# An attention and FFN kernel: the intermediate gh moved by 64 bytes, and a hand-written order for VectorE and ScalarE in the A stages

## The chip, the cores and the metric

One core of one Trainium2 chip. The metric is the device time of one execution in microseconds (us), the median of several runs. Five engines are named: TensorE (PE, with PEld for its weight loads), VectorE (DVE), ScalarE (ACT), GpSimd (POOL) and SyncE (SP), whose queue issues the DMAs.

## The reference

An attention over a small memory, and then a bilinear feed-forward:

```python
# q, k, v: (8 batches, 8 heads, 576, 64); phi: (8, 8, 576, 32)
a = softmax(phi, axis=2)                      # over the 576 positions
k_m = einsum('bhsm,bhsd->bhmd', a, k)         # 32 memory slots a head
v_m = einsum('bhsm,bhsd->bhmd', a, v)
attn = softmax(q @ k_m.T / sqrt(64)) @ v_m
x = attn.transpose(0, 2, 1, 3).reshape(4608, 512)
h = (x @ w1) * (x @ w2)                       # 1024 wide
out = (h @ w3) @ w_out                        # (4608, 512)
```

## The kernel before

All matmuls of the FFN work on numbers split in two fp32r halves, hi and lo, and use three products (hi·hi, lo·hi, hi·lo). `split` makes the halves: ScalarE casts the hi one, VectorE subtracts to get the lo one.

*Start.* w3 and w_out are multiplied once into W (1024x512; L493), kept as `Wh`, `Wl`.

*Attention of a batch* is cut into steps, each a generator in `attention(b)`. Heads are taken in pairs. `top` (L193) reduces `ph`, the transposed phi (two column groups t of 576), to the negated maxima `mx`. `exp` (L200) exponentiates `ph` and sums it. `norm` takes the reciprocals. `row` turns the maxima (L207), sends them to DRAM in four small DMAs (L210) and reads them back into all partitions as `all` (L212). `less` adds `all` to the rows of phi (L220, 128x1024, and L223) and exponentiates them (L226). Either these rows or, in early batches (b under `BY_ROWS` = 3), `ph` transposed on TensorE (`turn0` with eight transposes, L240, copied by ScalarE at L244; `turn4` with a ninth, L247, copied at L249) give the phi for `mem`, which multiplies it with k and v (L259, L268). Both parts of `turn` use the one PSUM tile `x`. `blocks` lays k_m and v_m out (L285 to L290). The scores, their softmax (`sc`, `se`, `sn`, `pr`) give the attention weights `ah`, `al`. `memory_weights` folds v_m into w1 and w2 and gives `mh`, `ml`, so that x is never formed.

*The A stage* of a batch: 16 units, one for each of 8 blocks f of 128 hidden features and 2 halves n of the 576 tokens. A unit is six matmuls of 288 columns into PSUM bank a (x @ w1) and six into bank b (x @ w2) (L583); a copy of a into `a_sb` on ScalarE (L597); the product `gr` = b · a_sb on VectorE (L600); and the split of `gr` into `gh[f]` (L131, ScalarE) and `gl[f]` (L133, VectorE). Banks a and b are two deep, as are `a_sb` and `gr`.

*The O stage*: for each 128 tokens 24 matmuls of 512 columns, `gh`, `gl` as weights and `Wh`, `Wl` moving (L612), a copy to `osb` (L624) and a DMA out. In all 36 blocks, so 864 matmuls. Odd batches use columns 0 to 575 of `gh` and `gl`, even batches those from 64 on.

*The order.* `START` orders the start and batch 0 step by step; then `SECOND` orders batch 1 and `STEADY` batches 2 to 7. A word is one step: `A` a unit, `O` a quarter of an output block, `top`, `less` and so on those steps for the next batch, with `+` for the one after that; `phi2`, `rows2`, `kv2` in batch 1 are loads for batch 3, and so on. TensorE and SP run always in the order of these tables. VectorE and ScalarE do so in `START` only; in `SECOND` and `STEADY` a scheduler that estimates times places their instructions. The tiles of the O and A stages (`gh`, `gl`, `a_sb`, `gr`, `turned`, `osb`) lie in pool `big`, one behind the other, `mx32` first.

Of the kernel before, what the change touches and what calls it, by code (L numbers as in the profile page):

```python
# [8 lines left out]
F32 = mybir.dt.float32  # L9
F32R = mybir.dt.float32r  # L10
# [3 lines left out]
AF = mybir.ActivationFunctionType  # L14
ALU = mybir.AluOpType
AX = mybir.AxisListType
# [27 lines left out]
pr0.1 O2 M3 M3 pr1.1 pr0.1 pr1.1 O3 O2 M3 O2 O3 O3 O3 O3 O3  # L44
""".split()
SECOND = """
phi2 A top exp A norm A turn0 A turn4 A mem rows2 A kv2 blocks A top+ row+ A exp+ A norm+ A A A A A less+ A A
mem+ sc0 sc1p Mp O kv3 se0 O se1 O q2 sn0 O pr0 O sn1 O pr1 M Mp Mp O O phi3 rows3 O O blocks+ O O O O O O Oo Oo Oo Oo
""".split()
STEADY = """  # L50
A top+ row+ A exp+ A norm+ A A A A A A A A less+ A A A A A
mem+ sc0 sc1p Mp O kv3 se0 O se1 O q2 sn0 O pr0 O sn1 O pr1 M Mp Mp O O phi3 rows3 O O blocks+ O O O O O O Oo Oo Oo Oo
""".split()

# [2 lines left out]
def memory_attention__then__bilinear_ffn_kernel(  # L57
# [19 lines left out]
    nc = tc.nc  # L77
    P = 128
    B, NG, S = qT.shape[0], 4, 576
    D = 64  # L80
    M = 32
    NT = 2
    DF = 1024
    weights = weights.bitcast(I32)
    NF = DF // P
    DO = 512
    HALF = S // 2
# [24 lines left out]
    for x, where in (("h", Wh), ("l", Wl)):  # L112
        t = const.tile([P, half, DO], F32R, name=f"W{x}0")
        where += [t[:, i] for i in range(half)]

    def psum(pool, name):
        return pool.tile([P, 512], F32, name=name, tag=name)

    def psum_pair():
        return ps_x.tile([P, 2, 512], F32, name="x")  # L120
# [9 lines left out]
    def split(hi, lo, src):  # L130
        nc.scalar.copy(out=hi, in_=src)  # L131
        yield
        nc.vector.tensor_tensor(out=lo, in0=src, in1=hi.bitcast(F32), op=ALU.subtract)  # L133

    def whole(step):
        for _ in step:
            pass
# [39 lines left out]
    def load(what, b):  # L177
        b += int(what[-1])
        if b < B:
            return LOADS[what[:-1]](b)  # L180
        return ()
# [4 lines left out]
    def attention(b):  # L186

        v = {}

        def top():  # L190
            v["ph"] = loaded.pop(("ph", b))
            v["mx"] = mx32[:, :NT] if b >= BY_ROWS else att.tile([P, NT], F32, name="mx")
            nc.vector.tensor_reduce(out=v["mx"], in_=v["ph"], axis=AX.X, op=ALU.max, negate=True)  # L193
            yield

        def exp():
# [18 lines left out]
        def less():  # L215
            a = loaded.pop(("rows", b))
            v["a"] = a.rearrange("p (c t x) -> p c t x", t=NT, x=P)
            x = a[:, : 8 * P].rearrange("p (c x) -> p c x", c=4)
            mx = v["all"].rearrange("p (c x) -> p c x", c=1)
            nc.vector.tensor_tensor(out=x, in0=x, in1=mx.broadcast_to([P, 4, NT * P]), op=ALU.add)  # L220
            for t in range(NT):
                x = a[t * D : (t + 1) * D, 8 * P : 9 * P]
                nc.vector.tensor_tensor(out=x, in0=x, in1=v["all"][t * D : (t + 1) * D, t * P : (t + 1) * P], op=ALU.add)  # L223
            yield
            a = a[:, : 9 * P]
            nc.scalar.activation(out=a, in_=a, func=AF.Exp)  # L226
            yield

        def norm():
            nc.vector.tensor_scalar_add(v["sm"], v["sm"], 1e-9)  # L230
# [114 lines left out]
        steps = {"top": top, "row": row, "less": less, "exp": exp, "norm": norm, "mem": memories, "blocks": blocks}  # L345
# [10 lines left out]
    def memory_weights(b):  # L356

        ms = ready["M", b] = {}

        def step(q, banks):  # L360
            one = None if banks else psum_pair()
            ps = banks() if banks else [one[:, t] for t in range(NT)]
            for g in range(NG):
                for t in range(NT):
                    d = slice((1 - t) * D, (2 - t) * D)
                    nc.tensor.matmul(  # L366
                        ps[t][g * M : (g + 1) * M],
                        lhsT=vm[b % 2][d, g],
                        rhs=w12_sb[q][d, :, g],
                        start=True,  # L370
                        stop=True,
                    )
            yield
            mh = const.tile([P, NT, 2, FQ], F32R, name=f"mh{q}", tag=f"m{m_tags[2 * q]}")
            ml = const.tile([P, NT, 2, FQ], F32R, name=f"ml{q}", tag=f"m{m_tags[2 * q + 1]}")
            ms[q] = mh, ml
            if banks:
                for t in range(NT):
                    yield from split(mh[:, t], ml[:, t], ps[t].rearrange("p (w f) -> p w f", w=2))
            else:  # L380
                yield from split(mh, ml, one.rearrange("p t (w f) -> p t w f", w=2))

        return [lambda banks=None, q=q: step(q, banks) for q in range(NQ)]


    tasks, at = [], 0
# [122 lines left out]
    def by_hand():  # L509
        return tc.manual_schedule(engines=set(HAND) | {mybir.EngineType.Activation, mybir.EngineType.DVE})  # L510

    BY_ROWS = 3
    steps = [attention(b) for b in range(B)]
    m0, m1 = memory_weights(0), memory_weights(1)
# [46 lines left out]
            for what in START[:cut]:  # L561
                go_on(what)
    big = ctx.enter_context(tc.tile_pool(name="big", bufs=1))
    mx32 = big.tile([P, M], F32, name="mx32")
    nc.gpsimd.memset(mx32, 0.0)

    REST = S % P
    gh, gl = [[big.tile([P, S + REST], F32R, name=f"g{x}{f}") for f in range(NF)] for x in "hl"]  # L570

    banks = {}

# [18 lines left out]
    def ab_unit(b, n, f, both=True):  # L592
        yield from ab_matmuls(b, n, f, 0)
        if both:
            whole(ab_matmuls(b, n, f, 1))
        a_sb = big.tile([P, HALF], F32, name="a_sb", bufs=2)
        nc.scalar.copy(out=a_sb, in_=banks.pop((b, n, f, 0)))  # L597
        yield
        gr = big.tile([P, HALF], F32, name="gr", bufs=2)
        nc.vector.tensor_tensor(out=gr, in0=banks.pop((b, n, f, 1)), in1=a_sb, op=ALU.mult)  # L600
        yield
        at = b % 2 * REST + n * HALF
        yield from split(gh[f][:, at : at + HALF], gl[f][:, at : at + HALF], gr)

    def out_block(b, i):

        first = 0 if b % 2 else REST
        at = first + i * P
        ps = psum(ps_o, "o")
        for f in range(NF):  # L610
            for k, (x, y) in enumerate(((gh, Wh), (gl, Wh), (gh, Wl))):
                nc.tensor.matmul(  # L612
                    ps,
                    lhsT=x[f][:, at : at + P],
                    rhs=y[f],
                    start=f == 0 and k == 0,
                    stop=f == NF - 1 and k == 2,
                )
            if f % 2:
                yield  # L620
        osb = big.tile([P, DO], F32, name="osb", bufs=2)
        c = b * S + at - b % 2 * REST
        if at == 0 or b + 1 < B or at + P < S:
            nc.scalar.copy(out=osb, in_=ps)  # L624
            yield
            if at:
                nc.sync.dma_start(out=out[c : c + P], in_=osb)
            else:
                for j in range(2):
                    c = (b - 1 + j) * S  # L630
                    nc.sync.dma_start(out=out[c : c + REST], in_=osb[j * REST : (j + 1) * REST])
        else:
            for j, copy in enumerate((nc.scalar.copy, nc.vector.tensor_copy)):
                x = slice(j * DO // 2, (j + 1) * DO // 2)
                copy(out=osb[:, x], in_=ps[:, x])
                nc.sync.dma_start(out=out[c : c + P, x], in_=osb[:, x])
# [2 lines left out]
        for what in START[cut:]:  # L639
            go_on(what)  # L640

    for b in range(1, B):
        ab = iter([(n, f) for f in range(NF) for n in range(2)])
        blocks = iter(range((S + b % 2 * REST) // P))
        m1 = iter(memory_weights(b + 1) if b + 1 < B else ())
        part, block = 0, None

        for what in (SECOND, STEADY)[b > 1]:
            if what == "A":
                whole(ab_unit(b, *next(ab)))  # L650
            elif what == "O" or what == "Oo":
                if what == "O" or b % 2:
                    if part == 0:
                        block = out_block(b, next(blocks))
                    part = (part + 1) % 4
                    next(block)
                    if part == 0:
                        whole(block)
            elif what[:-1] in LOADS:
                whole(load(what, b))  # L660
            elif what[-1] == "+":
                if b + 2 < B:
                    whole(steps[b + 2][what[:-1]]())
            elif b + 1 == B:
                pass
            elif what[0] == "M":
                whole(next(m1)(banks_ab if what == "Mp" else None))
            else:
                whole(steps[b + 1][what]())


_INS = ["qT", "kv", "phiT", "phi", "weights"]
# [64 lines left out]
```

## Time and profile before

| | us |
|---|---|
| median of 3 runs | 538.95 |
| lowest, highest | 538.88, 539.77 |
| profiled execution | 538.71 |
| its span (first to last instruction) | 536.9 |

In the profile, times are us from the start of the span; `a<-b` are the tiles written and read; a figure in square brackets is the idle time of the engine ahead of an instruction, with what ended it. Busy shares of TensorE, VectorE and ScalarE in 40 equal slices of the span (a digit is tenths):

```profile
PE   8999999999999999999999999999999999999997
DVE  4889997594569336773668245854676056905400
ACT  6998975543545225444544244344443144514310
```

The start takes the first five slices or so. After it, A and O stages alternate; the A stage of batch 2, for instance, runs from 192.66 to 219.00 us and that of batch 7 from 479.98 to 505.37.

### The profile page before, as it was taken

The numbers are of one execution on the slowest core, as the hardware profiler recorded it, in microseconds if no ns is written. First come the engines' busy times: TensorE is split into PE (matmuls) and PEld (weight loads), VectorE is DVE, ScalarE is ACT, GpSimd is POOL, SyncE is SP. The second block draws the span as 40 slices with busy tenths as digits, with TensorE's granted clock in tenths as the row PEclk, the third lists the DMA queues.
The fourth block names the chain that finished last, engine by engine and source line by source line (L and its number), as shares of the span: only waits on it lengthen the run. The fifth ranks groups of instructions, "written<-read, shape, count | busy, mean of one in ns | idle before, by whom it ended". The sixth has DMA issues, their size and how long they took to land.

```text
span 536.9 us, 9831 instructions
## 1 busy us (share of the span) xinstructions
PE 526.9 (98%) x4041; PEld 432.1 (80%) x4041; DVE 316.5 (59%) x614; ACT 252.0 (47%) x505; POOL 0.8 (0%) x7
## 2 busy tenths in 40 slices
PE   8999999999999999999999999999999999999997
PEld 5457678869986899868986899779976898689985
DVE  4889997594569336773668245854676056905400
ACT  6998975543545225444544244344443144514310
POOL 0000000000000000000000000000000000000000
PEclk9999999999999999999999999999999999999999
DMA  8999357252516310542034300730021100010011
GB/s 327 421 415 421 134 201 309 95 211 84 222 25 272 127 51 0 187 159 98 1 114 188 132 29 1 282 130 32 1 89 40 59 1 2 21 59 1 1 39 59
DMA packets 16460, 67.67 MB, mean 126 GB/s; under 512 B 1952, under 2 KB 2848, under 8 KB 11552
## 3 DMA queue, kind: packets, MB, share of 16 engines
q1 hardware_dynamic: 16416, 67.06, 32.7%
q8 instruction: 31, 0.51, 0.4%
q14 instruction: 13, 0.11, 0.1%
HBM read 57.61 MB, written 9.44 MB: 125 GB/s over the span
## 4 chain that ended last, share of the span: by engine, by line
PE 76%; DMA 12%; DVE 4%; issue 3%; ACT 2%; SPq 2%; ACTq 0%; DVEq 0%
PE o L612 36%; PE b L583 13%; PE a L583 12%; DMA kv<-in_weights 4%; DMA all<-mx 3%; PE a L366 2%; DMA mx<-turned 2%; PE a L493 2%; DMA ph<-in_phiT 2%; PE b L493 2%; PE o L259 2%; PE x L366 2%; DMA raw<-in_weights 1%; PE b L366 1%; PE x L259 1%
## 5 line engine op out<-in xcount | busy, mean ns | idle before, releaser
L600 DVE TENSOR_TENSOR gr<-b,a_sb 128x288 f32<-128x288 f32 x128 | 57.9, 456 | 82.9 <-PE b L583 78.0
L612 PE MATMUL o<-W,gh 128*128 128x512 f32 x288 | 97.6, 399 | 0.0
L131 ACT CAST gh<-gr 128x288 fp32r<-128x288 f32 x128 | 55.0, 432 | 87.7 <-DVE gr L600 87.5
L133 DVE TENSOR_TENSOR gl<-gr,gh 128x288 fp32r<-128x288 f32 x128 | 58.0, 456 | 46.7 <-ACT gh L131 45.5
L583 PE MATMUL b<-ah,mh 128*128 128x288 f32 x256 | 76.1, 297 | 2.7 <-DVE gr L600 2.6
L583 PE MATMUL a<-ah,ml 128*128 128x288 f32 x256 | 75.5, 295 | 0.4 <-DVE ml L133 0.4
L583 PE MATMUL a<-ah,mh 128*128 128x288 f32 x256 | 75.8, 296 | 0.0
L583 PE MATMUL a<-al,mh 128*128 128x288 f32 x256 | 75.6, 295 | 0.0
L583 PE MATMUL b<-al,mh 128*128 128x288 f32 x256 | 75.6, 295 | 0.0
L583 PE MATMUL b<-ah,ml 128*128 128x288 f32 x256 | 75.3, 294 | 0.0
L624 ACT COPY osb<-o 128x512 f32<-128x512 f32 x35 | 20.5, 587 | 112.4 <-PE o L612 99.4
L612 PEld LDWEIGHTS o<-W,gh 128*128 128x128 f32 x288 | 54.2, 188 | 18.2 <-issue 6.1
L612 PE MATMUL o<-Wh,gh 128*128 128x512 f32 x144 | 57.6, 400 | 0.0
L597 ACT COPY a_sb<-a 128x288 f32<-128x288 f32 x128 | 50.6, 395 | 14.0 <-PE a L583 13.8
L612 PE MATMUL o<-Wh,gl 128*128 128x512 f32 x144 | 56.9, 395 | 0.0
L612 PE MATMUL o<-Wl,gh 128*128 128x512 f32 x144 | 56.9, 395 | 0.0
L612 PE MATMUL o<-W,gl 128*128 128x512 f32 x144 | 56.7, 394 | 0.0
L583 PEld LDWEIGHTS b<-ah,mh 128*128 128x128 f32 x256 | 48.2, 188 | 5.0 <-DVE gr L600 4.1
L583 PEld LDWEIGHTS a<-ah,mh 128*128 128x128 f32 x256 | 48.2, 188 | 1.9 <-issue 1.0
L583 PEld LDWEIGHTS a<-ah,ml 128*128 128x128 f32 x256 | 48.1, 188 | 0.6 <-DVE ml L133 0.6
L583 PEld LDWEIGHTS a<-al,mh 128*128 128x128 f32 x256 | 48.1, 188 | 0.5
L583 PEld LDWEIGHTS b<-ah,ml 128*128 128x128 f32 x256 | 48.1, 188 | 0.0
(140 smaller groups left out, 771.0 us busy)
## 6 DMA issues: line engine op xcount, KB each, us to landing
kv<-in_kv SPq DMA_DIRECT2D x16, 1024.0 KB, 7.8
raw<-in_weights SPq DMA_DIRECT2D x10, 1024.0 KB, 16.3
q<-in_qT SPq DMA_DIRECT2D x8, 1152.0 KB, 8.2
out<-osb SPq DMA_DIRECT2D x31, 256.0 KB, 2.0
raw<-in_weights SPq DMA_DIRECT2D x12, 512.0 KB, 6.6
ph<-in_phiT SPq DMA_DIRECT2D x8, 576.0 KB, 10.1
kv<-in_weights SPq DMA_DIRECT2D x3, 1024.0 KB, 7.4
a<-in_phi SPq DMA_DIRECT2D x5, 576.0 KB, 4.8
```

The lines of the kernel that those rows point to most:

```text
L131: nc.scalar.copy(out=hi, in_=src)
L133: nc.vector.tensor_tensor(out=lo, in0=src, in1=hi.bitcast(F32), op=ALU.subtract)
L259: nc.tensor.matmul(ps[t][h * M : (h + 1) * M, : 2 * D], lhsT=v["a"][:, i, t, h * M : (h + 1) * M], rhs=kvt[i][:, (4 * t + h) * 2 * D : (4 ...
L366: nc.tensor.matmul(ps[t][g * M : (g + 1) * M], lhsT=vm[b % 2][d, g], rhs=w12_sb[q][d, :, g], start=True, stop=True,)
L493: nc.tensor.matmul(pw[r][i], lhsT=x[:, i * P : (i + 1) * P], rhs=y, start=k == 0 and j == 0, stop=k == NF - 1 and j == len(pairs) - 1,)
L583: nc.tensor.matmul(ps, lhsT=x[:, t, w, fc : fc + P], rhs=y[:, n, t * HALF : (t + 1) * HALF], start=i == 0, stop=i == len(todo) - 1,)
L597: nc.scalar.copy(out=a_sb, in_=banks.pop((b, n, f, 0)))
L600: nc.vector.tensor_tensor(out=gr, in0=banks.pop((b, n, f, 1)), in1=a_sb, op=ALU.mult)
L612: nc.tensor.matmul(ps, lhsT=x[f][:, at : at + P], rhs=y[f], start=f == 0 and k == 0, stop=f == NF - 1 and k == 2,)
L624: nc.scalar.copy(out=osb, in_=ps)
```

## The change

It has five parts.

1. `mx32` takes 48 words instead of 32, of which the first 32 are used. So `gh[0]` starts 64 bytes past a multiple of 512 instead of at one, and all the tiles behind it in the pool move by the same 64 bytes. W, `mh`, `ml`, `ah`, `al` stay where they are.
2. The order of the A stages of batches 1 to 7 is now by hand for VectorE and ScalarE too. `SECOND` and `STEADY` hold only these stages; the rest of each batch is in `REST` and stays with the scheduler. (The number once called `REST` is `REST_ROWS`.)
3. Within a stage, a unit emits its matmuls, `a_sb` and `gr`; then come the small attention steps that stand between this `A` and the next; then the cast to `gh` and the subtraction to `gl`.
4. Steps are cut smaller: `top` reduces each of its two groups by itself, with a stop between them from batch 2 on; `less` adds 512 columns at a time; its exponential is 640 and 512 columns instead of 1152.
5. In `SECOND`, `row+` stands ahead of the loads `rows2` and `kv2`, and `turn0`, `turn4`, `mem`, `blocks` of batch 2 come some units later. The `top` of batch 2 is no longer pulled into the start.

```diff
 SECOND = """
-phi2 A top exp A norm A turn0 A turn4 A mem rows2 A kv2 blocks A top+ row+ A exp+ A norm+ A A A A A less+ A A
-mem+ sc0 ...
+phi2 A top A top A exp A exp norm A turn0 top+ A turn0 turn4 top+ A turn4 row+ A mem rows2 kv2 A mem exp+
+A blocks exp+ norm+ A blocks A less+ A less+ A less+ A less+ A less+
 """.split()
 STEADY = """
-A top+ row+ A exp+ A norm+ A A A A A A A A less+ A A A A A
+A top+ A top+ A row+ exp+ A exp+ A norm+ A A A A A A less+ A less+ A less+ A less+ A less+ A
+""".split()
+REST = """
 mem+ sc0 sc1p Mp O kv3 se0 O ...
...
         def top():
...
-            nc.vector.tensor_reduce(out=v["mx"], in_=v["ph"], axis=AX.X, op=ALU.max, negate=True)
+            for t in range(NT):
+                nc.vector.tensor_reduce(out=v["mx"][:, t : t + 1], in_=v["ph"][:, t], axis=AX.X, op=ALU.max, negate=True)
+                if b > 1:
+                    yield
             yield
...
         def less():
...
-            nc.vector.tensor_tensor(out=x, in0=x, in1=mx.broadcast_to([P, 4, NT * P]), op=ALU.add)
+            for i in range(2):
+                x = a[:, 4 * P * i : 4 * P * (i + 1)].rearrange("p (c x) -> p c x", c=2)
+                nc.vector.tensor_tensor(out=x, in0=x, in1=mx.broadcast_to([P, 2, NT * P]), op=ALU.add)
+                yield
...
-            a = a[:, : 9 * P]
-            nc.scalar.activation(out=a, in_=a, func=AF.Exp)
-            yield
+            for x in (a[:, : 5 * P], a[:, 5 * P : 9 * P]):
+                nc.scalar.activation(out=x, in_=x, func=AF.Exp)
+                yield
...
-    mx32 = big.tile([P, M], F32, name="mx32")
+    mx32 = big.tile([P, M + M // 2], F32, name="mx32")[:, :M]
...
+        def go(what, step):
+            if by_steps:
+                if what not in begun:
+                    begun[what] = step()
+                next(begun[what], None)
+            else:
+                whole(step())
+
+        for what in order:
             if what == "A":
-                whole(ab_unit(b, *next(ab)))
+                whole(unit)
+                unit = ab_unit(b, *next(ab))
+                for _ in range(3):
+                    next(unit)
...
+    for b in range(1, B):
+        with by_hand():
+            run(b, (SECOND, STEADY)[b > 1], True)
+        run(b, REST, False)
```

Three places show what the order does to the instructions. In rows of the order, the number behind a tile's name tells buffers of one name apart.

VectorE at the start of batch 2's A stage, before; `mx_610`, `all` and `a` are those of the `top`, `row` and `less` of batch 4, and `gr`, `gl` the A units':

```order
L193 TENSOR_REDUCE mx_610<-ph 128x2
L207 STREAM_TRANSPOSE turned<-mx_610 128x32
L230 TENSOR_SCALAR sm<-sm 128x2
L231 RECIPROCAL sm<-sm 128x2
L600 TENSOR_TENSOR gr<-b,a_sb 128x288
L133 TENSOR_TENSOR gl_620<-gr,gh_612 128x288
L600 TENSOR_TENSOR gr<-b,a_sb 128x288
L133 TENSOR_TENSOR gl_620<-gr,gh_612 128x288
L600 TENSOR_TENSOR gr<-b,a_sb 128x288
L220 TENSOR_TENSOR a<-a,all 128x1024
L223 TENSOR_TENSOR a<-a,all 64x128 x2
L133 TENSOR_TENSOR gl_621<-gr,gh_613 128x288
```

The same stage after, first at its start and then from its eleventh unit:

```order
L607 TENSOR_TENSOR gr<-b,a_sb 128x288
L196 TENSOR_REDUCE mx_611<-ph 128x1
L135 TENSOR_TENSOR gl_621<-gr,gh_613 128x288
L607 TENSOR_TENSOR gr<-b,a_sb 128x288
L196 TENSOR_REDUCE mx_611<-ph 128x1
L135 TENSOR_TENSOR gl_621<-gr,gh_613 128x288
```

```order
L607 TENSOR_TENSOR gr<-b,a_sb 128x288
L226 TENSOR_TENSOR a<-a,all 128x512
L135 TENSOR_TENSOR gl_626<-gr,gh_618 128x288
L607 TENSOR_TENSOR gr<-b,a_sb 128x288
L226 TENSOR_TENSOR a<-a,all 128x512
L135 TENSOR_TENSOR gl_626<-gr,gh_618 128x288
```

The addition of `less` moved from behind the third unit to behind the eleventh, and is in pieces with a unit's `gl` and the next `gr` between them.

ScalarE in batch 1 where `turn` is copied out of PSUM, before and then after:

```order
L597 COPY a_sb<-a 128x288
L244 COPY a<-x 128x1024
L597 COPY a_sb<-a 128x288
L131 CAST gh_613<-gr 128x288
L249 COPY a<-x 128x128
```

```order
L133 CAST gh_615<-gr 128x288
L604 COPY a_sb<-a 128x288
L251 COPY a<-x 128x1024
L133 CAST gh_615<-gr 128x288
L604 COPY a_sb<-a 128x288
L256 COPY a<-x 128x128
```

The copy of the eight transposes now stands behind the `a_sb` of the unit that TensorE does after them; TensorE's ninth transpose follows that unit in both orders.

VectorE late in the start, while batch 0's A units run, before and then after:

```order
L133 TENSOR_TENSOR ml_944<-x,mh_943 128x1024
L133 TENSOR_TENSOR gl_623<-gr,gh_615 128x288
L193 TENSOR_REDUCE mx<-ph 128x2
L600 TENSOR_TENSOR gr<-b,a_sb 128x288
L133 TENSOR_TENSOR gl_627<-gr,gh_619 128x288
```

```order
L135 TENSOR_TENSOR ml_946<-x,mh_945 128x1024
L135 TENSOR_TENSOR gl_624<-gr,gh_616 128x288
L607 TENSOR_TENSOR gr<-b,a_sb 128x288
L135 TENSOR_TENSOR gl_628<-gr,gh_620 128x288
```

The reduction, the `top` of batch 2, is gone from this place.

More of the change, by code (lines that the diff above doesn't have):

```diff
@@ L46 @@
 SECOND = """
-phi2 A top exp A norm A turn0 A turn4 A mem rows2 A kv2 blocks A top+ row+ A exp+ A norm+ A A A A A less+ A A
-mem+ sc0 sc1p Mp O kv3 se0 O se1 O q2 sn0 O pr0 O sn1 O pr1 M Mp Mp O O phi3 rows3 O O blocks+ O O O O O O Oo Oo Oo Oo
+phi2 A top A top A exp A exp norm A turn0 top+ A turn0 turn4 top+ A turn4 row+ A mem rows2 kv2 A mem exp+
+A blocks exp+ norm+ A blocks A less+ A less+ A less+ A less+ A less+
 """.split()
 STEADY = """
-A top+ row+ A exp+ A norm+ A A A A A A A A less+ A A A A A
+A top+ A top+ A row+ exp+ A exp+ A norm+ A A A A A A less+ A less+ A less+ A less+ A less+ A
+""".split()
+REST = """
 mem+ sc0 sc1p Mp O kv3 se0 O se1 O q2 sn0 O pr0 O sn1 O pr1 M Mp Mp O O phi3 rows3 O O blocks+ O O O O O O Oo Oo Oo Oo
@@ L217, in less @@
             v["a"] = a.rearrange("p (c t x) -> p c t x", t=NT, x=P)
-            x = a[:, : 8 * P].rearrange("p (c x) -> p c x", c=4)
             mx = v["all"].rearrange("p (c x) -> p c x", c=1)
-            nc.vector.tensor_tensor(out=x, in0=x, in1=mx.broadcast_to([P, 4, NT * P]), op=ALU.add)
+            for i in range(2):
+                x = a[:, 4 * P * i : 4 * P * (i + 1)].rearrange("p (c x) -> p c x", c=2)
+                nc.vector.tensor_tensor(out=x, in0=x, in1=mx.broadcast_to([P, 2, NT * P]), op=ALU.add)
+                yield
             for t in range(NT):
@@ L563, in memory_attention__then__bilinear_ffn_kernel @@
     big = ctx.enter_context(tc.tile_pool(name="big", bufs=1))
-    mx32 = big.tile([P, M], F32, name="mx32")
+    mx32 = big.tile([P, M + M // 2], F32, name="mx32")[:, :M]
     nc.gpsimd.memset(mx32, 0.0)
-    REST = S % P
-    gh, gl = [[big.tile([P, S + REST], F32R, name=f"g{x}{f}") for f in range(NF)] for x in "hl"]
+    REST_ROWS = S % P
+    gh, gl = [[big.tile([P, S + REST_ROWS], F32R, name=f"g{x}{f}") for f in range(NF)] for x in "hl"]
     banks = {}
@@ L601, in ab_unit @@
         yield
-        at = b % 2 * REST + n * HALF
+        at = b % 2 * REST_ROWS + n * HALF
         yield from split(gh[f][:, at : at + HALF], gl[f][:, at : at + HALF], gr)
     def out_block(b, i):
-        first = 0 if b % 2 else REST
+        first = 0 if b % 2 else REST_ROWS
         at = first + i * P
@@ L621, in out_block @@
         osb = big.tile([P, DO], F32, name="osb", bufs=2)
-        c = b * S + at - b % 2 * REST
+        c = b * S + at - b % 2 * REST_ROWS
         if at == 0 or b + 1 < B or at + P < S:
@@ L630, in out_block @@
                     c = (b - 1 + j) * S
-                    nc.sync.dma_start(out=out[c : c + REST], in_=osb[j * REST : (j + 1) * REST])
+                    nc.sync.dma_start(out=out[c : c + REST_ROWS], in_=osb[j * REST_ROWS : (j + 1) * REST_ROWS])
         else:
@@ L640, in memory_attention__then__bilinear_ffn_kernel, with run @@
             go_on(what)
-    for b in range(1, B):
+    def run(b, order, by_steps):
+        m1 = iter(memory_weights(b + 1) if b + 1 < B and not by_steps else ())
         ab = iter([(n, f) for f in range(NF) for n in range(2)])
[L644 to L648, printed above, removed]
+        blocks = iter(range((S + b % 2 * REST_ROWS) // P))
+        begun, unit, part, block = {}, (), 0, None
+        def go(what, step):
[6 more added lines that the diff above has]
+        for what in order:
             if what == "A":
-                whole(ab_unit(b, *next(ab)))
+                whole(unit)
+                unit = ab_unit(b, *next(ab))
+                for _ in range(3):
+                    next(unit)
             elif what == "O" or what == "Oo":
@@ L662, in memory_attention__then__bilinear_ffn_kernel @@
                 if b + 2 < B:
-                    whole(steps[b + 2][what[:-1]]())
+                    go(what, steps[b + 2][what[:-1]])
             elif b + 1 == B:
@@ L668, in memory_attention__then__bilinear_ffn_kernel @@
             else:
-                whole(steps[b + 1][what]())
+                go(what, steps[b + 1][what])
+        whole(unit)
+    for b in range(1, B):
+        with by_hand():
+            run(b, (SECOND, STEADY)[b > 1], True)
+        run(b, REST, False)
 _INS = ["qT", "kv", "phiT", "phi", "weights"]
```

## The prediction

> **What bounds the kernel now.** I read the page first, then the waits, then windows cut at the A stages, then the instructions around each gap. The page has TensorE busy nearly throughout:
>
> ```profile
> PE 526.9 (98%) x4041; PEld 432.1 (80%) x4041; DVE 316.5 (59%) x614; ACT 252.0 (47%) x505; POOL 0.8 (0%) x7
> ```
>
> TensorE is the bound, at a granted clock of 1.00 in every window below. So the time falls only if TensorE stands less, or if one of its matmuls takes less. The change touches both: the hand order can remove stands, and the 64 bytes can only alter a matmul's (or another engine's) own duration. Of the waits, these two name the stand and, as I show next, its cause:
>
> ```profile
> DVE a L220 <- DMA all<-mx: 6.2, 5, 1.6
> PEld b L583 <- DVE gr L600: 4.1, 6, 1.1
> ```
>
> The columns are total us, times, and the longest. Six times a weight load for the first matmul into bank b waits for the product `gr` that must empty that bank: 4.1 us. Windows over the A stages of batches 1 to 7 show where (PE, weight load, VectorE, ScalarE busy; then clock, DMA):
>
> ```profile
> core 0: us, PE busy (x) PEld busy (x) DVE busy (x) ACT busy (x) POOL busy (x), PEclk, DMA share, GB/s
> 127.00:157.40 30.40, 29.57 (x286) 28.57 (x284) 17.09 (x41) 16.34 (x41) 0.00 (x0) 1.00 0.35 131
> 192.66:219.00 26.34, 25.76 (x194) 25.36 (x192) 14.99 (x33) 13.03 (x33) 0.00 (x0) 1.00 0.05 17
> 248.69:274.82 26.13, 25.74 (x193) 25.34 (x191) 14.98 (x33) 13.03 (x33) 0.00 (x0) 1.00 0.05 16
> 310.09:335.99 25.90, 25.76 (x194) 25.36 (x192) 14.99 (x33) 13.03 (x33) 0.00 (x0) 1.00 0.05 16
> 365.69:391.81 26.12, 25.73 (x194) 25.33 (x192) 14.90 (x33) 13.03 (x33) 0.00 (x0) 1.00 0.05 17
> 427.07:452.57 25.50, 25.50 (x194) 25.33 (x192) 13.74 (x30) 11.98 (x32) 0.00 (x0) 1.00 0.03 12
> 479.98:505.37 25.39, 25.39 (x194) 25.39 (x192) 13.64 (x30) 11.97 (x32) 0.00 (x0) 1.00 0.03 12
> ```
>
> Batches 6 and 7 have no attention steps beside their 192 matmuls and take 25.50 and 25.39 us. Batches 2 to 5 do the same 192 matmuls in 25.90 to 26.34. The excess is one hole each. Here is batch 2's, on VectorE and then TensorE:
>
> ```profile
> 199.51 1.23 DVE L220 TENSOR_TENSOR a<-a,all 128x1024 f32<-128x1024 f32 x1 [1.35 <-DMA all<-mx]
> 201.64 0.81 DVE L600 TENSOR_TENSOR gr<-b,a_sb 128x288 f32<-128x288 f32 x2
> ```
>
> ```profile
> 201.27 0.29 PE L583 MATMUL a<-ah,ml 128*128 128x288 f32 x1
> 202.15 0.40 PE L583 MATMUL b<-ah,mh 128*128 128x288 f32 x1 [0.58 <-DVE gr L600]
> ```
>
> VectorE stands 1.35 us at the addition of `less` until `all` lands, then does that step's work; two `gr`, one overdue, stand queued behind. At 132 ns a matmul (row `204.79` below) 202.15 should have been 201.40: 0.75 us lost, and about 0.10 more because the first matmul after a stand took 0.40 us instead of 0.29. START has the same hole behind the reduction of `top`, and batch 1 the largest behind `less`:
>
> ```profile
> 94.29 1.35 DVE L193 TENSOR_REDUCE mx<-ph 128x2 f32<-128x1152 f32 x1 [2.01 <-DMA ph<-in_phiT]
> 95.36 0.29 PE L583 MATMUL b<-ah,ml 128*128 128x288 f32 x1
> 96.07 0.40 PE L583 MATMUL b<-ah,mh 128*128 128x288 f32 x1 [0.41 <-DVE gr L600]
> ```
>
> ```profile
> 152.19 1.23 DVE L220 TENSOR_TENSOR a<-a,all 128x1024 f32<-128x1024 f32 x1 [1.60 <-DMA all<-mx]
> 153.70 0.29 PE L583 MATMUL a<-ah,ml 128*128 128x288 f32 x1
> 154.82 0.40 PE L583 MATMUL b<-ah,mh 128*128 128x288 f32 x1 [0.83 <-DVE gr L600]
> ```
>
> **The change part by part.**
>
> *Hand order, START.* The reduction that stood there belongs to batch 2; by hand it comes in batch 1's stage, long after its `ph` landed. The hole goes: 96.07 − 95.36 − 0.13 + 0.10 = 0.68 us.
>
> *Hand order, batch 1's `less`.* 154.82 − 153.70 − 0.13 + 0.10 = 1.09 us goes, if `all` is there in time. The column maxima now leave on the SP queue ahead of the loads of the rows and of kv for batch 3, after unit 7, and `less` starts after unit 12: five units, 7.9 us. What is late next is the load of the rows. In batch 2 the maxima took this on the queue:
>
> ```profile
> 193.94 1.15 SPq L210 DMA_DIRECT2D mx<-turned  x4
> 196.23 0.34 SPq L212 DMA_DIRECT2D all<-mx  x1
> ```
>
> and by the page a load of rows lands as the last column says (us):
>
> ```profile
> a<-in_phi SPq DMA_DIRECT2D x5, 576.0 KB, 4.8
> ```
>
> So the rows go out 196.57 − 193.94 = 2.6 us after the first of them and land 4.8 later: 7.4 of 7.9. I cost it at nothing, but at 1 us more for the load this stand would come back by half. The last exponential (640 and 512 instead of 1152) ends near the end of the stage, and the key-value products need it: 0 to 0.2 us, I take 0.1 lost.
>
> *Hand order, batches 2 to 5.* All four fall to the pace of 6 and 7, 25.45 on average: 0.89 + 0.68 + 0.45 + 0.67 = 2.69 us. As 25.50 stands among the undisturbed too, I take 2.6. Cover is needed here: each unit of 12 matmuls lasts 1.58 us, and beside it VectorE and ScalarE have these:
>
> ```profile
> L600 DVE TENSOR_TENSOR gr<-b,a_sb 128x288 f32<-128x288 f32 x128 | 57.9, 456 | 82.9 <-PE b L583 78.0
> L133 DVE TENSOR_TENSOR gl<-gr,gh 128x288 fp32r<-128x288 f32 x128 | 58.0, 456 | 46.7 <-ACT gh L131 45.5
> L131 ACT CAST gh<-gr 128x288 fp32r<-128x288 f32 x128 | 55.0, 432 | 87.7 <-DVE gr L600 87.5
> L597 ACT COPY a_sb<-a 128x288 f32<-128x288 f32 x128 | 50.6, 395 | 14.0 <-PE a L583 13.8
> L200 ACT ACTIVATE ph<-ph,mx 128x576 f32<-128x576 f32 x16 | 12.3, 770 | 1.0 <-DVE mx L193 0.9
> ```
>
> A half step on VectorE is 1.35/2 = 0.68 us (`top`) or 1.23/2 = 0.62 (`less`), with two 456 ns instructions 1.59; on ScalarE 0.77 with 0.43 and 0.40 is 1.60. Both are a hair over 1.58 as the rows stand, but consecutive instructions overlap (two `gr` in 0.81 us above), so about 1.45. At most two neighbouring units have such a step, and the next use of the same bank is 18 matmuls (2.4 us) after `gr` may start. So the halves hide, as do the 0.06 us or so that each split adds.
>
> *A new wait in batch 1.* The transposes of `turn` use one PSUM tile. Their second part must wait until ScalarE has copied the first. Before, the copy came ahead of the next unit's `a_sb`:
>
> ```profile
> 132.95 1.02 ACT L244 COPY a<-x 128x1024 f32<-128x1024 f32 x1 [1.16 <-PE x L240]
> 133.87 0.40 ACT L597 COPY a_sb<-a 128x288 f32<-128x288 f32 x1
> 134.37 0.27 PE L247 MATMUL x<-ident,ph 128*128 128x128 f32 x1
> 193.67 0.40 ACT L597 COPY a_sb<-a 128x288 f32<-128x288 f32 x1 [0.17 <-PE a L583]
> ```
>
> By hand it stands behind that `a_sb`, which starts some 0.2 us after its bank is full. Counted from the bank's last matmul: `a_sb` to about 0.55, the copy to 1.57. TensorE arrives at the second part after bank b, 0.13 + 0.79 = 0.92. It stands 0.65 us, and every later matmul of TensorE is queued behind.
>
> *Sum of the order:* 0.68 + 1.09 + 2.6 − 0.1 − 0.65 = 3.6 us saved.
>
> *The address.* `gh`, `gl` and the small tiles behind them move by 64 bytes; W, `mh`, `ml`, `ah` stay. The 864 output matmuls read `gh` or `gl` as weights against moving W, and no run has them at the new distance. By where the tiles lie, W starts 128 past a multiple of 512, `gh` now 0 or 256, then 64 or 320. The nearest rows are other matmuls of 512 columns:
>
> ```profile
> 505.53 27.89 PE o L612 x120
> 161.56 8.60 PE o L612 x36
> 43.36 0.39 PE L493 MATMUL o<-woh,ah 128*128 128x512 f32 x1
> 49.71 0.39 PE L493 MATMUL a<-wo,m 128*128 128x512 f32 x1
> 60.12 0.63 PE L493 MATMUL a<-al,m 128*128 128x512 f32 x2
> 62.22 0.63 PE L493 MATMUL o<-al,m 128*128 128x512 f32 x2
> 204.79 0.79 PE a L583 x6
> ```
>
> An output matmul takes 27.89/120 = 232.4 ns in the last batch, 238.9 in batch 1's first stretch. The weight products take (49.71 − 43.36)/28 = 226.8 while all their tiles lie at the same place modulo 512, and (62.22 − 60.12)/9 = 233.3 when two in three have their tiles 64 bytes apart. So a distance may matter by some ns, and the nearest row (64 apart) says +0.9 ns, or +0.8 us. Against it: the A matmuls also mix tiles 64 apart and run 132 ns without unevenness. I take 0. The ends are 226.8 (−5.6 ns × 864 = −4.8 us) and 238.9 (+6.5 ns, +5.6 us).
>
> The Trainium skill, "TensorE: Matmul & The Clock Gate", section "Step-by-step: what each phase is for", gives TensorE two independent read ports, one for the weights and one for the moving tile; by that no address could slow or speed a matmul, and the sum would stay 3.6 us. The three different times above for one shape leave room for doubt, since the rule explains none of them.
>
> **Sum.** The profiled execution took 538.71 us (span 536.9), 0.24 under the median of 538.95. 538.71 − 3.6 = 535.1; against the median 535.35. I say 535.3.
>
> **The rivals.**
>
> *The address speeds the output matmuls.* For it: 226.8 ns at the same shape, and 132 ns for 288 columns lies on one line with 226.8 for 512 (0.42 ns a column), while 232.4 lies above it. Against: `gh` at 0 and at 256, in even and odd batches, already differ in address and not in pace. Full effect 535.3 − 4.8 = 530.5; half of it 532.9.
>
> *The order brings half.* A DVE or ACT order that is fixed cannot step around a late DMA; a row load later than 7.9 us in batch 1, or a stage that still stands at a half step leaves, say, half of 3.6: 537.1. Against: `all` has several units more room than before.
>
> *Slower: the address costs.* Place: the output matmuls; price 864 × x. At x = 4.2 ns the order's gain is gone, at 5.4 ns (3.6 + 1.08 us) the kernel is slower by 0.2%; at 238.9 ns it is 535.3 + 5.6 = 540.9. For it: that stretch shows such a pace exists (beside other traffic, its cause not visible). Against: the 64-apart row is 233.3.
>
> *No effect.* The hand order moves the stands elsewhere, to the `turn` copy above all, or the address costs about 4 ns: 538 to 539.5.
>
> **How the numbers follow.** What this kernel's measurement can tell from no change is about 0.2%, 1.08 us: under 537.87 is faster, over 540.03 slower. Chances: order as computed and address within 1 ns (534.2 to 536.4) 0.45; address gains 0.25; order half 0.15; no effect 0.08; slower 0.07. The likeliest gives 535.3. Faster is the first two and nearly all of the third, 0.84; same 0.09; slower 0.07. The range from 530.4 (full address gain) to 537.8 leaves out the last two and a little beyond the gain, under 0.2.
>
> **What the next profile would show.** The waits of weight loads of b for `gr` near zero; the A stages of batches 2 to 5 at 25.4 to 25.5; no gap near 95; in batch 1 a stand of about 0.65 us at the transpose after unit 6, and none of 1 us behind `less`; the last 120 output matmuls in 27.9 us. If those take 27.2, the address helps; 28.5 or more, it eats the gain. The forecast is wrong if the stretches of output matmuls change at all, or if VectorE still stands for `all`.

## The result, and the profile after

The changed kernel takes 532.02 us (531.87 to 532.25) against 538.91 for the kernel before on the same chip: a ratio of 0.9871, 95% interval 0.9854 to 0.9888. The forecast was 535.3 us with a range of 530.4 to 537.8. The profiled execution has a span of 530.1 us where the one before had 536.9, so 6.8 us are to be found.

The engines' line of the page, and then two of TensorE's waits (total us, times, longest):

```profile
PE 523.4 (99%) x4041; PEld 432.7 (82%) x4041; DVE 315.8 (60%) x627; ACT 252.3 (48%) x510; POOL 0.8 (0%) x7
```

```profile
PEld x L254 <- ACT a L251: 1.1, 2, 0.9
PEld b L590 <- issue: 0.8, 1, 0.8
```

The wait of bank b for `gr`, 4.1 us before, is no longer in the list, nor is VectorE's for `all`; a weight load for bank b of an A unit stands only once more, for 0.8 us, and for no other engine. The new wait is that of the ninth transpose for ScalarE's copy. The windows of the A stages of batches 1 to 7, in the columns of the prediction's table:

```profile
125.73:157.94 32.21, 31.55 (x364) 30.38 (x370) 19.83 (x49) 18.42 (x47) 0.00 (x0) 1.00 0.34 124
190.68:216.15 25.47, 25.47 (x193) 25.30 (x192) 16.64 (x39) 14.57 (x38) 0.00 (x0) 1.00 0.05 17
245.52:271.00 25.48, 25.48 (x194) 25.31 (x192) 16.64 (x39) 14.66 (x38) 0.00 (x0) 1.00 0.06 17
305.86:331.33 25.47, 25.47 (x193) 25.30 (x192) 16.73 (x39) 14.68 (x38) 0.00 (x0) 1.00 0.04 16
360.70:386.18 25.48, 25.48 (x194) 25.31 (x192) 16.73 (x39) 14.68 (x38) 0.00 (x0) 1.00 0.05 17
421.04:446.51 25.47, 25.47 (x193) 25.30 (x192) 13.65 (x30) 11.98 (x32) 0.00 (x0) 1.00 0.03 12
473.55:498.93 25.38, 25.38 (x194) 25.37 (x192) 13.64 (x30) 11.98 (x32) 0.00 (x0) 1.00 0.03 12
```

Batches 2 to 5 now run at the pace of 6 and 7, though VectorE and ScalarE do more in them than before (VectorE 16.64 against 14.99 us in batch 2: `top`, `row`, `norm` and on ScalarE `exp` now fall inside the stage; `less` and its exponential did so before, too). The first window reaches further than the one shown before, to the end of that stage's key-value products; the pair with equal ends, batch 1 from its first A matmul to its first output matmul, is this, before and then after:

```profile
127.13:161.49 34.36, 33.53 (x413) 31.20 (x411) 19.45 (x46) 17.61 (x44) 0.00 (x0) 1.00 0.35 126
```

```profile
125.73:159.91 34.18, 33.52 (x413) 31.18 (x411) 20.97 (x52) 19.05 (x49) 0.00 (x0) 1.00 0.36 129
```

Only 0.18 us came of it, for the hole of 1.1 us behind `less` was traded for this one, on TensorE and then on ScalarE:

```profile
136.01 0.29 PE L590 MATMUL b<-ah,ml 128*128 128x288 f32 x1
136.97 0.33 PE L254 MATMUL x<-ident,ph 128*128 128x128 f32 x1 [0.66 <-ACT a L251]
```

```profile
135.60 0.40 ACT L604 COPY a_sb<-a 128x288 f32<-128x288 f32 x1 [0.75 <-PE a L590]
135.89 1.02 ACT L251 COPY a<-x 128x1024 f32<-128x1024 f32 x1
```

The copy ends at 136.91 and the transpose starts 0.06 later; in step it would have started at 136.14, so TensorE lost 0.83 us. In the start, the 42 matmuls of batch 0 around the old hole behind `top`, before and after:

```profile
91.52:97.76 6.24, 5.83 (x44) 5.60 (x42) 3.55 (x7) 1.65 (x5) 0.00 (x0) 1.00 0.13 52
```

```profile
91.11:96.65 5.54, 5.54 (x43) 5.54 (x42) 2.27 (x6) 1.64 (x5) 0.00 (x0) 1.00 0.17 68
```

And the last 120 output matmuls, which took 27.89 us (chain, start and us):

```profile
499.09 27.49 PE o L619 x120
```

That is 229.1 ns each instead of 232.4. Over all output matmuls that start less than 300 ns behind the one before (819 of them) the mean from start to start went from 232.6 to 229.1, in odd and even batches alike; 864 × 3.5 ns = 3.0 us. The A matmuls stayed at 132 ns, six in

```profile
195.59 0.79 PE a L590 x6
```

| where | us won |
|---|---|
| START up to the first A unit (65.92 to 65.48) | 0.44 |
| START, the hole behind `top` (6.24 to 5.54) | 0.70 |
| batch 1 to its first output matmul | 0.18 |
| A stages of batches 2 to 5 (104.49 to 101.90) | 2.59 |
| A stages of 6 and 7 | 0.04 |
| output matmuls, 864 × 3.5 ns | 3.0 |
| sum | 6.95, of 6.8 |

The first row is no effect of the change: over all profiles below, the first A unit starts between 64.97 and 66.45 us with no order in it.

### The profile page after: what moved, and what is told of

Its sections match the earlier page's. It is cut to its first block, busy times and chain, and to the rows that moved or that the text cites. A ratio compares the mean times of both kernels' runs of the same rounds, so it can differ in the third digit from the quotient of the medians.

```text
span 530.1 us, 9856 instructions
## 1 busy us (share of the span) xinstructions
PE 523.4 (99%) x4041; PEld 432.7 (82%) x4041; DVE 315.8 (60%) x627; ACT 252.3 (48%) x510; POOL 0.8 (0%) x7
## 4 chain that ended last, share of the span: by engine, by line
PE 86%; DVE 6%; ACT 3%; DMA 3%; issue 1%; SPq 0%; DVEq 0%; ACTq 0%
PE o L619 38%; PE a L590 19%; PE b L590 19%; DMA raw<-in_weights 3%; PE a L373 2%; PE o L266 2%; PE x L373 2%; DVE w L454 2%; PE b L373 1%; ACT u L450 1%; PE x L308 1%; PE x L266 1%; DVE w L452 1%; DVE m L484 1%; ACT w L444 1%
```

## The experiments

**The two halves apart.** The 64 bytes alone, on the kernel before:

```diff
-    mx32 = big.tile([P, M], F32, name="mx32")
+    mx32 = big.tile([P, M + M // 2], F32, name="mx32")[:, :M]
```

> The kernel before with mx32 of 48 words alone: gh, gl and the tiles behind them 64 bytes on, the order untouched. Theory (the address is worth about 3.5 ns an output matmul, 864 of them, and nothing else): 538.9 - 3.0 = 535.9 us, output matmuls of the last stretch 229 ns instead of 232.4, and the holes behind less and top still there. Rival (the output matmuls became faster because the hand order takes VectorE's and ScalarE's traffic from beside them): no change, 538.9 us and 232.4 ns.

Measured: 536.14 us against 539.31, ratio 0.9947 (0.9927 to 0.9968). The last 120 output matmuls and the waits of the old order:

```profile
501.87 27.49 PE o L612 x120
```

```profile
DVE a L220 <- DMA all<-mx: 6.2, 5, 1.7
PEld b L583 <- DVE gr L600: 4.0, 6, 1.1
```

The pace of the changed kernel, with every hole of the old one. The rival falls: traffic of the other engines is not it.

The order alone, the changed kernel with

```diff
-    mx32 = big.tile([P, M + M // 2], F32, name="mx32")[:, :M]
+    mx32 = big.tile([P, 32], F32, name="mx32")[:, :M]
```

> The changed kernel with mx32 of 32 words again: the hand order alone. Theory: the order is worth 3.5 us (START 0.7, batch 1 0.2, batches 2 to 5 2.6), so 535.4 us, and output matmuls at 232.4 ns. Rival (order and address act on each other, the hand order saving only what the address leaves): the two parts do not add up to 6.9, this run above 536.5 or below 534.

Measured: 535.14 us, ratio 0.9929 (0.9917 to 0.9942); 120 output matmuls again in

```profile
502.35 27.89 PE o L619 x120
```

So 3.2 us from the address and 4.2 from the order by these medians, 7.3 together where the whole change gave 6.9: they add up within the spread of the start.

**Which place.** Only the words of `mx32` change (64, 80, 40, 56 for `gh` at 128, 192, 32, 96). In one run, called both moved, `mx32` has its 32 words again and a tile ahead of W takes 64 bytes more, so that W and every tile behind it, `gh` too, lie 64 bytes further:

```diff
-    vm = [const.tile([P, NG, M], F32, name=f"vm{i}") for i in range(2)]
+    vm = [const.tile([P, NG * M + 16 * i], F32, name=f"vm{i}")[:, : NG * M].rearrange(...) for i in range(2)]
```

> The changed kernel with mx32 of 64 words: gh and gl 128 bytes past a multiple of 512, where W lies too; even batches read 256 bytes further. Theory A (the distance between weights and moving tile modulo 512 counts, equal is best): 226.8 ns an output matmul in odd batches, as in the weight products, and more in even ones. Theory B (a place at an odd multiple of 64 bytes is what helps, any multiple of 128 is alike): 232.4 ns in all, the time back at 535.0 us. Theory C (only places at multiples of 256 are slow): 229 ns or less in all, 532 us or less.

> The changed kernel with W and all tiles from there on 64 bytes further: W at 192 past a multiple of 512, gh at 64, so their distance is that of the kernel before (128) and gh's own place that of the changed one. Theory (the distance between the weights' and the moving tile's places counts): 232.4 ns an output matmul in the last stretch, about 535 us. Rival (gh's own place counts): 229 ns, about 532 us.

> The changed kernel with gh at 192 past a multiple of 512, 64 above W instead of 64 below. Theory that only the size of the distance counts, with a period of 256 bytes (as even batches, which read gh 256 bytes further, keep the odd ones' pace): 229 ns. Rival (the further the place, the faster): 226 ns or less. Rival (the sign counts): above 230 ns.

> The changed kernel with gh at 32 past a multiple of 512, 96 below W. Theory (a smooth loss that grows with the distance): between 229.0 and 232.4 ns, about 230.7. Rival (places in steps of 64): 229 or 232.4 exactly.

> The changed kernel with gh at 96 past a multiple of 512, 32 below W. After 232.3 ns an output matmul in the last stretch at 128 below W, 233.4 at 96 below, 228.9 at 64 below, 227.0 at the same place and 233.3 at 64 above: theory (multiples of 64 below W are good, what lies between is bad): about 233 ns, 536 us. Rival (near is good): between 227.0 and 228.9 ns, 531.5 us.

The last 120 output matmuls, in the chain of the five, in this order (same place; both moved; gh at 192; at 32; at 96):

```profile
498.17 27.25 PE o L619 x120
```

```profile
501.59 27.89 PE o L619 x120
```

```profile
502.51 28.00 PE o L619 x120
```

```profile
503.05 28.01 PE o L619 x120
```

```profile
502.06 28.01 PE o L619 x120
```

| gh less W, bytes | W at | ns, 120 output matmuls | us |
|---|---|---|---|
| −128 (the order alone) | 128 | 232.4 | 535.14 |
| −128 (both moved) | 192 | 232.4 | 534.78 (one run) |
| −96 | 128 | 233.4 | 536.63 (one run) |
| −64 (the change) | 128 | 229.1 | 532.02 |
| −32 | 128 | 233.4 | 535.37 (one run) |
| 0 | 128 | 227.1 | 530.59 |
| +64 | 128 | 233.3 | 535.82 (one run) |

(The kernel before took 538.91 to 539.31 us beside these. The total of a single run is not to be read to 1 us; the readings here rest on the times of the matmuls.) With `gh` at 64 but W moved by as much, the gain is gone and even the run of single gaps is the old one to a nanosecond (228, 230, 233, 241, 232, 231, 232 ns over and over). So it is the distance between the weights' place and the moving tile's that counts, not the place of `gh`. It is not smooth (−32 is as bad as −96), and it has a sign (+64 is bad, −64 good). Even batches read `gh` and `gl` 256 bytes further than odd ones and keep their pace to 0.5 ns (batches 1 to 5) in every run, so 256 bytes more or less make no difference.

Of the theories, A had the pace of the same place right, but not that even batches would be slower. B is refuted there. C fits that run as well and falls with the run at 192, no multiple of 256 and yet 233.3 ns. At 192, the theory of the size alone and the rival of the further place are wrong, and the one of the sign holds. At 32, both my smooth theory and its rival are wrong. At 96, the theory held. What makes −64 good and −32, −96 and +64 bad stays open.

The same place gave 530.59 us, ratio 0.9841 (0.9828 to 0.9854), 1.4 us less than the change; the runs of the two do not overlap.

**The new stand in batch 1.** The second part of `turn` one unit later:

```diff
-phi2 A top A top A exp A exp norm A turn0 top+ A turn0 turn4 top+ A turn4 row+ A mem rows2 kv2 A mem exp+
+phi2 A top A top A exp A exp norm A turn0 top+ A turn0 top+ A turn4 row+ A turn4 mem rows2 kv2 A mem exp+
```

> The changed kernel with the second part of turn one unit later in batch 1, so that ScalarE's copy of the eight transposes is done when TensorE comes to the ninth. Theory (the stand of 0.82 us at that transpose is on the path): 532.0 - 0.8 = 531.2 us, no gap at the transpose. Rival (a stand gained back later, at the key-value products or the last exponential of batch 1): within 0.2 us of 532.0.

Measured: 531.40 us, ratio 0.9862 (0.9847 to 0.9876). By medians 0.6 less, though the intervals overlap; the trace is plainer. The window of batch 1 as above:

```profile
125.93:159.21 33.28, 33.28 (x413) 31.18 (x411) 21.00 (x52) 19.08 (x49) 0.00 (x0) 1.00 0.38 131
```

TensorE is busy through all 33.28 us; 34.18 − 33.28 = 0.90 us, and nothing takes its place. Against the kernel before, 34.36 − 33.28 = 1.08 us: the whole hole behind `less`.

**Size or place of the steps.** `top` and `less` uncut, with the code of the kernel before, in the changed kernel's tables:

> The changed kernel with top and less uncut: one reduction of 1152, one addition of 1024 with the two small ones behind it, one exponential of 1152, at the first of their places in the hand order. Theory (the place counts, not the size: a unit may be up to 0.8 us late before TensorE must wait, 2.4 of room less 1.6 of a unit): the reduction makes a unit's VectorE work 0.40 + 1.35 + 0.40 = 2.15 us, 0.6 late, hidden; less makes it 0.4 + 1.8 + 0.4 = 2.6, 1.0 late, 0.2 over the room; so 0 to 0.3 us in each of five stages, 532.0 to 533.5 us. Rival (small steps are what the hand order lives on): a stand of 0.5 us or more at each top and each less, over 535 us.

Measured: 531.92 us, ratio 0.9869 (0.9852 to 0.9885): the time of the change. Batch 2's A stage, and VectorE at its whole `less`:

```profile
190.33:215.80 25.47, 25.47 (x193) 25.31 (x191) 15.99 (x37) 14.22 (x37) 0.00 (x0) 1.00 0.05 17
```

```profile
208.05 0.46 DVE L602 TENSOR_TENSOR gr<-b,a_sb 128x288 f32<-128x288 f32 x1 [0.17 <-PE b L585]
208.43 1.22 DVE L222 TENSOR_TENSOR a<-a,all 128x1024 f32<-128x1024 f32 x1
210.17 0.46 DVE L135 TENSOR_TENSOR gl<-gr,gh 128x288 fp32r<-128x288 f32 x1
210.55 0.45 DVE L602 TENSOR_TENSOR gr<-b,a_sb 128x288 f32<-128x288 f32 x1
```

The next `gr` starts 2.50 us after the one ahead of it instead of 1.58, and TensorE does not feel it. Cutting reductions and additions was worth nothing here.

**Hand order with the old tables.** The kernel before, with only

```diff
-        for what in (SECOND, STEADY)[b > 1]:
+        order = (SECOND, STEADY)[b > 1]
+        mid = order.index("mem+")
...
+                hand = by_hand() if at == 0 else nullcontext()
```

> The kernel before, with VectorE and ScalarE by hand in the A stages of batches 1 to 7 but the old tables, whole steps and the old sequence in a unit (gh and gl straight behind gr); gh at its old place. To be set beside the order alone, 535.1 us. Theory (what cost time was the scheduler's pulling of less and top ahead of gr while a DMA was under way; order by the tables ends that): the holes of START and of batches 2 to 5 at less go; VectorE idles for each cast, and a whole less adds 1.8 us, so up to 0.7 us a stage may come back: 535 to 538 us. Rival (the new sequence and cut steps are needed, hand order alone brings nothing): 538.9 us or more.

Measured: 551.90 us, ratio 1.0238 (1.0223 to 1.0253), slower by 12.8. The theory's 535 to 538 us is refuted; the rival's range has no upper end, but a loss was in neither account. A wait that neither had:

```profile
PEld a L583 <- ACT a_sb L597: 13.2, 9, 1.8
```

ScalarE and TensorE in batch 2, at `less+`:

```profile
216.09 0.43 ACT L131 CAST gh<-gr 128x288 fp32r<-128x288 f32 x1 [0.85 <-DVE gr L600]
218.68 1.16 ACT L226 ACTIVATE a<-a 128x1152 f32<-128x1152 f32 x1 [2.16 <-DVE a L223]
219.75 0.38 ACT L597 COPY a_sb<-a 128x288 f32<-128x288 f32 x1
```

```profile
218.37 0.29 PE L583 MATMUL b<-ah,ml 128*128 128x288 f32 x1
220.18 0.40 PE L583 MATMUL a<-ah,mh 128*128 128x288 f32 x1 [1.52 <-ACT a_sb L597]
```

In a fixed order ScalarE stands 2.16 us for VectorE's additions, does the exponential, and only then the `a_sb` for which TensorE's bank a waits. I had looked at VectorE alone. The two exponentials of `exp+` cost 1.1 us in each stage in the same way.

The same, with the unit's new sequence (the steps ahead of the cast; the changed kernel's `run`, old tables, whole steps):

> VectorE and ScalarE by hand with the old tables and whole steps, gh at its old place, but with the new sequence in a unit: the steps between gr and the cast to gh of the same unit. It differs from the hand order with old tables (551.9 us) by that sequence alone, and from the order alone (535.1 us) by tables and step sizes. In the 551.9 us kernel TensorE stands 1.1 us behind the two exponentials of exp+ and 1.7 behind less+ in each of batches 2 to 5, in both cases for an a_sb queued behind them on ScalarE. Theory (the parts of a step must stand a unit apart, whatever the sequence): exp+ puts 1.9 us beside a_sb and cast in one unit, and less+ still puts an exponential behind an addition that has just begun, so most of the 3 us a stage stays: 545 to 552 us. Rival (the sequence in the unit is what counts, since a_sb of the next unit no longer waits for steps behind gl): 535 to 539 us.

Measured: 539.98 us, ratio 1.0006 (0.9990 to 1.0023): no different from the kernel before. Both theories missed: the first by 5 us, the rival by 1. The stand behind `exp+` is gone; of the wait there is left

```profile
PEld a L584 <- ACT a_sb L598: 4.5, 4, 1.1
```

four times, once in each of batches 2 to 5, behind `less+`, where the exponential still follows its additions at one place:

```profile
211.51 1.17 ACT L227 ACTIVATE a<-a 128x1152 f32<-128x1152 f32 x1 [2.48 <-DVE a L224]
212.58 0.41 ACT L132 CAST gh<-gr 128x288 fp32r<-128x288 f32 x1
212.90 0.39 ACT L598 COPY a_sb<-a 128x288 f32<-128x288 f32 x1
```

So of the 16.8 us between hand order with old tables and the order alone (551.90 and 535.14), the new sequence in a unit brought 11.9 and the new tables with the cut steps 4.8. Of the 4.8, 4.5 is the wait just shown, and the cuts were worth nothing above, so it is the places that count. They matter where a step passes from VectorE to ScalarE: `less` is whole in the run of 531.92 us too, but its exponential is called a unit later, when the additions are done.

**Both gains together**: `gh` at W's place, and the second part of `turn` a unit later.

> gh at 128 as W, and the second part of turn a unit later. Theory (the two gains add): 530.6 - 0.7 = 529.9 us, faster than both kernels by 2 to 9 us. Rival (the turn stand is gained back elsewhere once output matmuls are faster): 530.6 us.

Measured: 529.61 us (529.21 to 530.27), ratio 0.9825 (0.9812 to 0.9839), the best of all; the gains add, as forecast (529.9).

## Why the prediction was right or wrong

- *The sum and the time*: the time fell by 6.9 us where 3.65 were forecast. The order's half came as computed; the other half is the address, which the sum had at 0. That 532.02 us lies in the range is owed to the bound set for a rival, not to the sum, and so it is luck. By the prediction's own sign (wrong "if the stretches of output matmuls change at all") that step failed: they went from 232.4 to 229.1 ns.
- *What bounds the kernel, and the six holes*: right. All six are gone, and batches 2 to 5 gave 2.59 us where I took 2.6; START gave 0.70 where I had 0.68.
- *Batch 1's `less`*: right in kind. The load of the rows came in time, but not by the working given. On SP's queue, and then on VectorE:

```profile
139.62 1.16 SPq L215 DMA_DIRECT2D mx<-turned  x4
142.90 0.36 SPq L174 DMA_DIRECT2D a<-in_phi  x1
```

```profile
150.18 0.67 DVE L226 TENSOR_TENSOR a<-a,all 128x512 f32<-128x512 f32 x1
```

The rows went out 3.3 us behind the first of the maxima, not 2.6; with 4.8 to land (an estimate from the row of before) that is 8.1, more than the 7.9 allowed. It hid because `less` began 10.6 us behind, for the key-value products of batch 2 stand between those five units and the prediction had not counted them. That this term was nothing is luck, too. The new stand at `turn` was foreseen in its place and cause, and put at 0.65 us; it took 0.83. Counted from the start of the bank's last matmul (135.21 us), `a_sb` started at 0.39 where I had 0.2, the copy ended at 1.70 instead of 1.57, and the transpose began 0.06 later; TensorE would have come at 0.93, as I had it. Batch 1 gave 0.18 us net, where the terms made 0.34: the stand cost 0.90 in all instead of 0.65, and the 0.1 for the last exponential was not lost.

- *Sum of the order*: 3.6 us forecast, 3.5 found in the trace (0.70 + 0.18 + 2.59), 4.2 by the medians of the order alone.
- *The address*: this term was mis-sized, and it is the step that failed. I took 0 within −4.8 and +5.6; it is −3.0. The row I called nearest, weight products with two in three at 64 bytes' distance, 233.3 ns, misled: at −64 throughout, an output matmul takes 229.1. The other row I had was the better guide, for the tiles that lie at one place: 226.8 there, 227.1 here once `gh` lies where W does. That a mixture of distances should run slower than either of its parts is not explained by these runs.
- *The slow end of the address* was misread. The 238.9 ns "in batch 1's first stretch" are 8.60 us over 36 matmuls, but no pace; before, that stretch begins and ends so:

```profile
161.49 0.50 PE L612 MATMUL o<-Wh,gh 128*128 128x512 f32 x1
161.82 0.39 PE L612 MATMUL o<-Wh,gl 128*128 128x512 f32 x1
169.76 0.40 PE L612 MATMUL o<-Wl,gh 128*128 128x512 f32 x1
```

The second start comes 0.33 us after the first, and the 8.60 us hold the last matmul's whole 0.40 us, too. Between, 34 starts take 7.94 us, 233.5 ns each. No row showed a pace of 238.9, and no distance tried averaged more than 233.4.

- *The rival that came true in part* is the one in which the address speeds the output matmuls (0.25); half its effect was put at 532.9, and 532.02 was measured. "`gh` at 0 and at 256 differ in address and not in pace" was no evidence against it, since 256 bytes made no difference in any run. That 132 ns for 288 columns and 226.8 for 512 lie on one line was no evidence for it, since any two points do.
- *The rule weighed*: the Trainium skill, "TensorE: Matmul & The Clock Gate", section "Step-by-step: what each phase is for", gives TensorE two independent read ports. What the prediction drew from this, that no place could matter, does not hold here: the same matmuls took 227.1 to 233.4 ns, by where their operands lie relative to each other. Whether the ports have a part in it, no run here shows.
- *That halves hide*: right, but the cuts were not needed for it, as the whole steps show.

## What to carry to other kernels

When TensorE is busy 98% of the span, as here, look at the gap between its matmuls for each form: two forms of one shape that differ by a few ns may differ only in where their tiles lie, and a padding of some words between them tells. An order by hand is as good as its weakest queue: before fixing one, ask for each engine what stands behind every instruction that will wait, and put the second engine's part of a step a unit later than the first's. A step that fits the room of a double buffer need not be cut: a whole `less` cost nothing here.

## What the runs showed that I had not expected

The time of a matmul with 512 moving columns and new weights each time hangs on the distance of the two tiles' addresses: 227.1 ns at the same place, 229.1 with the weights 64 bytes below, 232.4 at 128 below, 233.3 to 233.4 at 32 or 96 below and at 64 above; a further 256 bytes make no difference. Whether the 288-column matmuls of the A stage have such a place is not shown, for no run changed the distance of their tiles; they took 132 ns in every run. And one change of who orders two engines, with no instruction added or taken away, moved this kernel from 539.1 to 551.9 us.
